# Spatial-stage z1 blocks loaded one quad ahead and gated inside the quad; LayerNorm squares of four rows sent behind the first copies of the z1 quads

## The chip, the cores and the metric

The kernel runs on one core of one Trainium2 chip. The metric is device time in microseconds (us), lower is better. Timed executions of the kernel before took 697.17, 697.22, 698.55 and 698.75 us. The profile is a trace of one execution. That execution has a time of its own.

## The reference, cut to what matters

```python
g = sigmoid((x * gate_w).sum(-1, keepdims=True))
a = attention(x, wqkv, wo)            # 32 heads, 8 keys each, 2 apart
z = gelu(x @ w_in)                    # 2048 x 3584
z1, z2 = z[..., :1792], layernorm(z[..., 1792:])
s = w_sp @ z2 + b_sp[:, None]         # the "spatial" product, 2048 x 2048 x 1792
b = (z1 * s) @ w_out
return g * a + (1 - g) * b
```

The kernel folds the factor `(1 - g)` into z1 before the last product. It calls this gating.

## The kernel before

Order of the work on TensorE (PE): the z2 columns and q, k, v; then 7 pairs of "z1 quads"; then 14 "spatial quads" (two halves `c` of 7); then 8 output quads. A quad is one level of Strassen's scheme: seven block products that accumulate in four PSUM banks. ScalarE (ACT) copies banks to seed others, VectorE (DVE) makes the operand sums and evicts the results. Quads alternate between two sets of four banks.

```python
def strassen(...):
    X, Y, Z, V = bank_roles[quad[0] % 2]
    ...
    product(X, A11 x B11);              nc.scalar.copy(Y, X)      # "first copy"
    product(V, S1 x T1);                share(vs, V)
    product(Y, S2 x T2);                nc.scalar.copy(Z, Y)
    product(X, A12 x B21);              c11(X)
    product(Y, S3 x T3);                nc.scalar.copy(V, Y); c22(Y)
    product(Z, S4 x B22);               c12(Z)
    product(V, A22 x T4);               c21(V)
```

Ahead of the z1 quads there are four dummy matmuls. They write banks 1, 2, 5 and 6, each of which must first be emptied by a GELU of the z2 columns (in the profile of before two of them waited 4.3 us for these). LayerNorm needs the sums of squares of z2. Those of rows 12 to 15 (tiles of 128 rows) are written in the program behind the z1 quads, but they have no order of their own, and the compiler placed them among the last GELUs of the z2 columns (in the profile of before they start from 289.94 to 302.02 us, the GELUs end at 301.9):

```python
for b in (1, 2, 5, 6):
    nc.tensor.matmul(banks[b], xT[:, 4, 0:P], xT[:, 4, 0:512], start=True, stop=True)
for fp in range(NFH):
    ...                                                          # cut
    run(z1_quad(fp, 0), z1_quad(fp, 1), hooks=...)
    if fp < 4:
        junk = free(A_OFF + 16384, FH)      # scratch: shares memory with a block of v that DVE reads
        for x in range(2):
            nc.scalar.activation(junk[...], z2[:, 12 + fp, x * HF:(x + 1) * HF], ACT.Square, accum_out=s2h[...])
```

The spatial quad, where a z1 block is loaded, gated in place, multiplied with the quad's result and stored from the same slot (two slots in turn):

```python
def spatial_quad(c, fp):
    n = quad[0]
    z1t, zgt, zt, vs = z1_slots[n % 2], zg_slots[n % 2], zt_slots[n % 2], v_slots[n % 2]
    for a in range(2):
        sync.dma_start(z1t[:, :, a, :], src)                     # z1 load
    first = sums4(...)                                           # operand sums of this quad
    with tc.high_priority():
        gated = nc.vector.tensor_tensor(zgt, z1t, om, ALU.mult)  # the gate
    if c == 1 and fp == 0:
        wsp_sums(1, 1)              # the last two of the weight sums: T2 and T4 of the second half
    ...
    def c11(X): nc.vector.tensor_tensor(zt[:, 0, 0, :], X[:], b1, ALU.add)
    ...                             # c22, c12 and c21: additions, products with zgt, then four stores
```

Between the spatial quads of the first half, pairs of transposing loads fetch the spatial weights of the second half through the same DMA queue.

Of the kernel before, what the change touches and what calls it, by code (L numbers as in the profile page):

```python
# [9 lines left out]
F32 = mybir.dt.float32  # L10
# [3 lines left out]
P = 128  # L14
# [11 lines left out]
FH = 1792  # L26
NF = FH // P
# [8 lines left out]
HF = FH // 2  # L36
NFH = NF // 2
# [5 lines left out]
A_OFF = X_OFF + 16384  # L43
# [10 lines left out]
def kernel(  # L54
# [13 lines left out]
    nc = tc.nc  # L68
# [4 lines left out]
    sm = ctx.enter_context(tc.tile_pool(name="small", bufs=1))  # L73
# [19 lines left out]
    z1_d = dpool.tile([4, P, NF * 512], BF, name="z1_d")  # L93
# [14 lines left out]
    g_att = sm.tile([P, NJ], F32, name="g_att")  # L108
    s1 = sm.tile([P, 64], F32, name="s1")
    s2 = sm.tile([P, 16], F32, name="s2")  # L110
    s2h = sm.tile([P, 8], F32, name="s2h")
    mean = sm.tile([P, 16], F32, name="mean")
    var = sm.tile([P, 16], F32, name="var")
    rstd = sm.tile([P, 16], F32, name="rstd")
# [274 lines left out]
    def square(i):  # L389
        inst = nc.scalar.activation(junk, z2[:, i, :], ACT.Square, accum_out=s2[:, i:i + 1])  # L390
        tc.add_manual_dep(inst.ins, last_evac[0].ins.name, NOSYNC, reason="behind the banded evacuations")

    def normalize(i):
        sl = slice(i, i + 4)
        s1v = s1[:, 4 * i:4 * (i + 4)].rearrange("p (i c) -> p i c", c=4)
        first = nc.vector.tensor_reduce(mean[:, sl], s1v, AX.X, ALU.add)
        tc.add_manual_dep(first.ins, last_add[0].ins.name, NOSYNC, reason="behind the additions of the quads")
        nc.vector.tensor_scalar(mean[:, sl], mean[:, sl], 1.0 / FH, None, ALU.mult)
        nc.vector.tensor_tensor(var[:, sl], mean[:, sl], mean[:, sl], ALU.mult)
        nc.vector.scalar_tensor_tensor(var[:, sl], s2[:, sl], 1.0 / FH, var[:, sl], ALU.mult, ALU.subtract)  # L400
        nc.vector.tensor_scalar(var[:, sl], var[:, sl], 0.0, EPS, ALU.max, ALU.add)
        nc.gpsimd.tensor_tensor(rstd[:, sl], var[:, sl], cm05[:, sl], ALU.pow)
        for ii in range(i, i + 4):
            nc.vector.tensor_scalar(z2h[:, ii, :], z2[:, ii, :], mean[:, ii:ii + 1], rstd[:, ii:ii + 1],
                                    ALU.subtract, ALU.mult)

    for i in range(16):
        if i > 5:
            for c in range(1, 4):
                z2_tile(i, c)  # L410
        if i < 12:
            square(i)

    def free(off, n, dt=BF):
        r = reg(off, n)
        return r if dt == BF else r.bitcast(dt)
# [35 lines left out]
    def strassen(A11, A12, A22, S1, S2, S3, S4, B11, B21, B22, T1, T2, T3, T4, vs, c11, c12, c21, c22, share=nc.scalar.copy):  # L452

        X, Y, Z, V = bank_roles[quad[0] % 2]
        bank_roles[quad[0] % 2] = [X, Z, V, Y]
        quad[0] += 1
        product(X, list(zip(A11, B11)), True)
        nc.scalar.copy(Y[:], X[:])  # L458
        yield
        product(V, list(zip(S1, T1)), True)  # L460
        with tc.high_priority():
            share(vs, V[:])  # L462
        yield
        product(Y, list(zip(S2, T2)), False)
        nc.scalar.copy(Z[:], Y[:])  # L465
        yield
        product(X, list(zip(A12, B21)), False)
        with tc.high_priority():
            c11(X)
        yield  # L470
        product(Y, list(zip(S3, T3)), False)
        seed = nc.scalar.copy(V[:], Y[:])  # L472
        with tc.high_priority():
            tc.add_manual_dep(c22(Y).ins, seed.ins.name, SYNC, reason="one reader of a bank at a time")
        yield
        product(Z, list(zip(S4, B22)), False)
        with tc.high_priority():
            c12(Z)
        yield
        product(V, list(zip(A22, T4)), False)  # L480
        with tc.high_priority():
            c21(V)
        yield

    def run(*quads, hooks={}):
        quads = list(quads)
        n = 0
        while quads:
            n += 1
            if n in hooks:  # L490
                hooks[n]()
            for q in list(quads):
                if next(q, 0) == 0:
                    quads.remove(q)
# [8 lines left out]
        return first  # L503

    last_add = [None]
    last_share = [None]
    last_store = [None]
    wait_for = [None, None, None]
# [21 lines left out]
    def x_sums(r):  # L530
        for c in range(2):
            lo, hi = slice(512 * c, 512 * c + 512), slice(1024 + 512 * c, 1536 + 512 * c)
            a, b = ((xT[:, 0:4, hi], xT[:, 0:4, lo]), (xT[:, 4:8, hi], xt1[:, :, lo]),
                    (xT[:, 4:8, hi], xT[:, 0:4, hi]), (xT[:, 4:8, lo], xt2[:, :, lo]))[r]
            with tc.high_priority():
                inst = nc.vector.tensor_tensor((xt1, xt2, xt3, xt4)[r][:, :, lo], a, b, ALU.subtract)
            if r == 0:
                tc.add_manual_dep(inst.ins, last_sub[0].ins.name, NOSYNC, reason="behind the softmax maxima")
            if r == 3:
                tc.add_manual_dep(inst.ins, last_share[0].ins.name, NOSYNC, reason="behind the shared terms")  # L540
# [14 lines left out]
    def z1_quad(fp, c):  # L555
        w, s, z1s, vs = w1_slots[fp % 3], ws_slots[fp % 2], z1s_slots[c], zv_slots[c]
        lo, hi = slice(512 * c, 512 * c + 512), slice(1024 + 512 * c, 1536 + 512 * c)

        def share(*a):
            last_share[0] = nc.vector.tensor_copy(*a)  # L560

        def gelu(f, a, bank):
            return nc.scalar.activation(z1s[:, f, a, :], bank[:], ACT.Gelu_apprx_tanh)  # L563

        def add(bank):
            last_add[0] = nc.vector.tensor_tensor(bank[:], bank[:], vs, ALU.add)
            return last_add[0]

        def c22(Y):
            inst = add(Y)  # L570
            gelu(1, 1, Y)
            return inst

        def c12(Z):
            add(Z)
            gelu(0, 1, Z)

        def c21(V):
            gelu(1, 0, V)
            for a in range(2):  # L580
                dst = z1_d[c + 2 * a].rearrange("p (f t) -> p f t", f=NF)[:, fp:fp + NFH + 1:NFH, :]
                last_store[0] = sync.dma_start(dst, z1s[:, :, a, :])

        K4 = range(4)
        return strassen([w[:, k, 0, :] for k in K4], [w[:, 4 + k, 0, :] for k in K4], [w[:, 4 + k, 1, :] for k in K4],
                        *[[s[:, q, k, :] for k in K4] for q in range(4)],
                        [xT[:, k, lo] for k in K4], [xT[:, 4 + k, lo] for k in K4], [xT[:, 4 + k, hi] for k in K4],
                        [xt1[:, k, lo] for k in K4], [xt2[:, k, lo] for k in K4], [xt3[:, k, lo] for k in K4],
                        [xt4[:, k, lo] for k in K4], vs, lambda X: gelu(0, 0, X), c12, c21, c22, share=share)

    for fp in range(3):
        load_w1(fp)
    w1_sums(0)
# [4 lines left out]
    for fp in range(NFH):  # L598
        if fp + 1 < NFH:
            w1_sums(fp + 1)  # L600
        for a in ((), (0,), (1, 2), (3, 4), (5, 6), (7,), ())[fp]:
            load_raw(0, a)
        if fp == 6:
            wsp_sums(0, 0)
        run(z1_quad(fp, 0), z1_quad(fp, 1), hooks={2: lambda: x_sums(2), 4: lambda: x_sums(3)} if fp == 0 else {})
        if fp < 4:
            junk = free(A_OFF + 16384, FH)
            for x in range(2):
                nc.scalar.activation(junk[:, x * HF:(x + 1) * HF], z2[:, 12 + fp, x * HF:(x + 1) * HF], ACT.Square,  # L609
                                     accum_out=s2h[:, 4 * x + fp:4 * x + fp + 1])  # L610
        if 1 <= fp <= 4:
            if fp == 4:
                nc.vector.tensor_tensor(s2[:, 12:16], s2h[:, 0:4], s2h[:, 4:8], ALU.add)
            normalize(4 * fp - 4)
        if fp + 3 < NFH:
            load_w1(fp + 3)

    def spatial_quad(c, fp):
        n = quad[0]
        raw = raw_slots[c].rearrange("p i a t -> p i (a t)")  # L620
        half, t_sum = raw_bits[c], t_sums[c]
        z1t, zgt, zt, vs = z1_slots[n % 2], zg_slots[n % 2], zt_slots[n % 2], v_slots[n % 2]
        for a in range(2):
            src = z1_d[c + 2 * a].rearrange("p (f t) -> p f t", f=NF)[:, fp:fp + NFH + 1:NFH, :]
            sync.dma_start(z1t[:, :, a, :], src)
        lo, hi = slice(fp * P, (fp + 1) * P), slice(HF + fp * P, HF + (fp + 1) * P)
        s = s_slots[n % 2]
        first = sums4([s[:, r] for r in range(4)], z2h[:, 0:8, lo], z2h[:, 8:16, lo], z2h[:, 0:8, hi], z2h[:, 8:16, hi])
        om = _sub_ap(omg_bc, 512 * c, [[0, 2], [1024, 2], [1, 512]])
        with tc.high_priority():  # L630
            gated = nc.vector.tensor_tensor(zgt, z1t, om, ALU.mult)  # L631
        if c == 1 and fp == 0:
            wsp_sums(1, 1)
        if c == 1 and fp == 1:
# [1 line left out]
        b1, b2 = bsp_bc[:, 512 * c:512 * c + 512], bsp_bc[:, 1024 + 512 * c:1536 + 512 * c]  # L636

        def c11(X):
            nc.vector.tensor_tensor(zt[:, 0, 0, :], X[:], b1, ALU.add)

        def c22(Y):
            nc.vector.tensor_tensor(vs, vs, b2, ALU.add)
# [184 lines left out]
```

## Time and profile before

| | kernel before |
|---|---|
| timed executions | 697.17 to 698.75 us |
| the profiled execution | 704.6 us (span 702.8 us) |
| PE busy in the profile | 681.7 us, 97% of the span |
| PE idle ahead of the z1 quads | 4.3 us |
| PE idle in the first quad of the second spatial half | 4.5 us |

The page of the profile of before: the totals by engine (busy us, share of the span, instructions), then the rows of PE's busy tenths and of its granted clock, in 40 slices of the span.

```profile
span 702.8 us, 9358 instructions
PE 681.7 (97%) x3623; PEld 320.8 (46%) x3623; DVE 407.1 (58%) x551; ACT 313.7 (45%) x563; POOL 6.1 (1%) x15
...
PE   6999999999999999889999999997999999999997
...
PEclk9999999999999999989999999998999999999999
```

PE is the bound, busy for 97% of the span: only its idle or slow time can be won. Both rows show dips near slices 17 to 18 and 28. The view of waits of the kernel before names them (engine, what it wrote, line, what it waited for: us in total, times, longest):

```profile
PE psum_all L201 <- DMA arena<-in_A_x_dram: 6.1, 2, 3.6
PE psum_all L449 <- DVE arena L523: 4.5, 1, 4.5
PE psum_all L597 <- ACT arena L223: 4.3, 2, 3.3
```

L597 is the line of the dummies, L223 the z2 GELUs, L523 the last weight sum. A table of windows of the kernel before shows the price of the idle time (columns: stretch in us; its length; busy us and instructions of PE, PE's weight loads, DVE, ACT and POOL; granted clock; DMA share; GB/s):

```profile
296.00:300.00 4.00, 0.66 (x4) 0.22 (x3) 3.64 (x4) 3.91 (x13) 0.00 (x0) 0.90 0.79 223
300.00:304.00 4.00, 2.99 (x7) 0.87 (x7) 0.16 (x1) 3.19 (x9) 0.00 (x0) 0.50 0.00 0
304.00:308.00 4.00, 4.00 (x15) 1.62 (x14) 1.11 (x2) 0.98 (x2) 0.00 (x0) 0.75 0.00 0
484.00:488.00 4.00, 0.16 (x1) 0.00 (x0) 3.96 (x5) 0.00 (x0) 0.00 (x0) 0.86 0.82 263
488.00:492.00 4.00, 3.37 (x8) 1.20 (x9) 4.00 (x7) 0.00 (x0) 0.00 (x0) 0.50 0.98 273
492.00:496.00 4.00, 4.00 (x16) 1.69 (x15) 4.00 (x8) 0.57 (x1) 0.00 (x0) 0.78 0.79 255
```

The clock is the column after POOL's. Around each stall the granted clock is 0.50 for 6.83 us (299.16 to 305.99 and 486.90 to 493.72): the first matmuls of the quads start 0.43 us apart, at full clock 0.216.

The timeline of ACT in the kernel before, around the first stall (start us, length us, engine, line, operation; in brackets the idle time ahead of it and what ended that):

```profile
282.61 0.54 ACT L223 ACTIVATE arena<-psum_all 128x448 bf16<-128x448 f32 x1
...
289.94 0.95 ACT L609 ACTIVATE arena<-arena 128x896 bf16<-128x896 bf16 x1 [6.70 <-issue]
...
291.82 0.52 ACT L223 ACTIVATE arena<-psum_all 128x448 bf16<-128x448 f32 x1
...
292.47 0.95 ACT L609 ACTIVATE arena<-arena 128x896 bf16<-128x896 bf16 x1
...
301.36 0.53 ACT L223 ACTIVATE arena<-psum_all 128x448 bf16<-128x448 f32 x1
...
302.02 0.95 ACT L609 ACTIVATE arena<-arena 128x896 bf16<-128x896 bf16 x1
```

ACT stands still for 6.7 us ahead of the first square (L609). "issue" means that the profile saw nothing to wait for, but the square does wait: its semaphore wait lasts 7.37 us and ends when DVE finishes its 4.42 us product that started at 285.44, the last reader of the memory that the scratch shares. Nine GELUs are then behind, with squares between them.

The timeline of DVE in the kernel before, around the second stall:

```profile
476.43 0.68 DVE L639 TENSOR_TENSOR arena<-psum_all,arena 128x512 f16<-128x512 f32 x1
482.02 1.23 DVE L631 TENSOR_TENSOR arena<-arena 128x2048 f16<-128x2048 bf16 x1 [4.92 <-DMA arena<-z_d]
483.17 0.68 DVE L643 TENSOR_TENSOR arena<-psum_all,arena 128x512 f16<-128x512 f32 x1
...
485.69 0.68 DVE L650 TENSOR_TENSOR arena<-psum_all,arena 128x512 f16<-128x512 f32 x1
486.30 2.28 DVE L523 TENSOR_TENSOR arena<-arena 128x4096 f16<-128x4096 bf16 x1
```

L631 is the gate. It waits 4.9 us for its z1 load, in front of evictions and the weight sum L523 (2.28 us). The first of those evictions, L643, belongs to the quad before: the copy that it follows was made at 470.44, some 12 us earlier, so DVE is almost a quad late. PE ran out of work at 484.16, waiting for that sum.

### The profile page before, as it was taken

To read this page: it belongs to the slowest core of one execution; us is meant where nothing else is said; L and a number is where in the kernel's file an instruction comes from. 1 tells how busy PE (TensorE), PEld (TensorE's weight loads), DVE (VectorE), ACT (ScalarE), POOL (GpSimd) and SP (SyncE) were. 2 spreads that over 40 slices of the span, in tenths; PEclk is the share of its full clock that TensorE was granted. 3 is DMA by queue.
4 is the path that set the end of the run, shared out by engine and by line. 5 is a ranking of instruction groups with operands and counts; after the bars stand their busy time and mean duration, and the time that the engine had idled before them with its cause. 6 is when DMAs were issued, how large, how long until landed. Compare 5 with 4: busy or idle time off the path is not lost.

```text
span 702.8 us, 9358 instructions
## 1 busy us (share of the span) xinstructions
PE 681.7 (97%) x3623; PEld 320.8 (46%) x3623; DVE 407.1 (58%) x551; ACT 313.7 (45%) x563; POOL 6.1 (1%) x15
## 2 busy tenths in 40 slices
PE   6999999999999999889999999997999999999997
PEld 3546544645444455434444444443444444444443
DVE  1000171977699969945677965497767694523301
ACT  4436457564768799666666311211111211112121
POOL 1000000000000000000010000000000000000000
PEclk9999999999999999989999999998999999999999
DMA  9995557485588570107986368838555388964200
GB/s 226 219 273 154 148 173 214 125 233 128 178 245 224 145 160 1 53 23 197 207 212 177 110 135 151 156 83 237 148 120 162 100 195 191 190 145 98 55 35 30
DMA packets 241740, 106.45 MB, mean 151 GB/s; under 512 B 189712, under 2 KB 235168, under 8 KB 241696
## 3 DMA queue, kind: packets, MB, share of 16 engines
q1 hardware_dynamic: 241008, 105.33, 60.1%
q8 instruction: 28, 0.46, 0.3%
q10 hardware_dynamic: 688, 0.53, 0.2%
q14 instruction: 16, 0.13, 0.1%
HBM read 45.10 MB, written 45.00 MB: 128 GB/s over the span
## 4 chain that ended last, share of the span: by engine, by line
PE 73%; DVE 9%; DMA 8%; SPq 4%; ACT 3%; issue 2%; DVEq 0%; ACTq 0%
PE psum_all L449 41%; PE psum_all L256 15%; PE psum_all L263 8%; PE psum_all L221 7%; DMA arena<-z_d 3%; SPq L188 3%; DVE arena L340 2%; PE psum_all L292 2%; DVE arena L631 1%; SPq L183 1%; DMA band_d_73<-arena 1%; ACT arena L609 1%; ACT arena L223 1%; DMA band_d_75<-arena 1%; DMA arena<-in_A_x_dram 1%
## 5 line engine op out<-in xcount | busy, mean ns | idle before, releaser
L449 PE MATMUL psum_all<-arena 128*128 128x512 f16 (+1 forms) x1792 | 392.2, 382 | 4.8 <-DVE arena L523 4.5
L449 PEld LDWEIGHTS <-arena 128*128 128x128 f16 (+1 forms) x1792 | 176.2, 98 | 222.2 <-issue 8.7
L256 PE MATMUL psum_all<-arena 128*128 128x512 bf16 x512 | 116.2, 380 | 0.0
L221 PE MATMUL psum_all<-arena 128*128 128x448 bf16 (+1 forms) x512 | 101.4, 357 | 0.4 <-ACT arena L223 0.4
L340 DVE TENSOR_TENSOR arena<-arena,att_A 128x8192 f16<-128x8192 bf16 x16 | 70.7, 4421 | 6.3 <-DMA arena<-v_d 6.1
L256 PEld LDWEIGHTS <-arena 128*128 128x128 bf16 x512 | 47.5, 98 | 56.6 <-issue 0.2
L221 PEld LDWEIGHTS <-arena 128*128 128x128 bf16 x512 | 49.7, 99 | 47.5 <-issue 2.6
L340 DVE TENSOR_TENSOR arena<-arena 128x4096 f16<-128x4096 f16 (+2 forms) x48 | 67.3, 1402 | 1.4
L297 ACT CAST arena<-psum_all 128x1620 f16<-128x1620 f32 (+2 forms) x48 | 65.1, 1356 | 3.7 <-DMA band_d_73<-arena 2.4
L458 ACT COPY psum_all<-psum_all 128x512 f32<-128x512 f32 x36 | 20.5, 570 | 89.3 <-PE psum_all L449 72.2
L263 PE MATMUL psum_all<-arena 128*128 128x512 bf16 x256 | 57.5, 381 | 0.0
L258 ACT CAST arena<-psum_all 128x512 bf16<-128x512 f32 x64 | 37.3, 586 | 40.6 <-PE psum_all L256 39.1
L465 ACT COPY psum_all<-psum_all 128x512 f32<-128x512 f32 x36 | 20.5, 570 | 53.6 <-PE psum_all L449 53.6
L263 PEld LDWEIGHTS <-arena 128*128 128x128 bf16 x256 | 36.1, 145 | 18.1
L472 ACT COPY psum_all<-psum_all 128x512 f32<-128x512 f32 x36 | 20.5, 571 | 50.2 <-PE psum_all L449 50.2
L223 ACT ACTIVATE arena<-psum_all 128x448 bf16<-128x448 f32 x64 | 34.4, 545 | 17.7 <-PE psum_all L221 17.7
L498 DVE TENSOR_TENSOR arena<-arena 128x512 f16<-128x512 bf16 (+2 forms) x37 | 20.6, 564 | 34.9 <-DMA arena<-zg_d 17.1
L563 ACT ACTIVATE arena<-psum_all 128x512 bf16<-128x512 f32 x56 | 31.8, 598 | 6.9 <-PE psum_all L449 3.6
L501 DVE TENSOR_TENSOR arena<-arena 128x512 f16<-128x512 bf16 (+2 forms) x37 | 20.5, 562 | 23.7 <-PE psum_all L449 13.0
L631 DVE TENSOR_TENSOR arena<-arena 128x2048 f16<-128x2048 bf16 x14 | 17.1, 1223 | 29.3 <-DMA arena<-z_d 28.6
L266 ACT CAST arena<-psum_all 128x512 bf16<-128x512 f32 x32 | 18.6, 585 | 26.3 <-PE psum_all L263 26.3
L462 ACT COPY arena<-psum_all 128x512 f32<-128x512 f32 x22 | 12.8, 587 | 36.2 <-PE psum_all L449 33.3
(86 smaller groups left out, 346.7 us busy)
## 6 DMA issues: line engine op xcount, KB each, us to landing
arena<-v_d SPq DMA_DIRECT2D x8, 960.0 KB, 6.0
z_d<-arena SPq DMA_DIRECT2D x28, 256.0 KB, 2.6
arena<-z_d SPq DMA_DIRECT2D x28, 256.0 KB, 3.5
zg_d<-arena SPq DMA_DIRECT2D x56, 128.0 KB, 2.3
arena<-zg_d SPq DMA_DIRECT2D x32, 224.0 KB, 3.4
arena<-in_A_wqkv_dram SPq DMA_DIRECT2D x16, 256.0 KB, 4.7
v_d<-arena SPq DMA_DIRECT2D x32, 128.0 KB, 2.6
o_d<-arena SPq DMA_DIRECT2D x4, 1024.0 KB, 5.8
```

Of the source, the lines that this page charges most:

```text
L188: inst = _orig_dmat(*a, **k)
L221: nc.tensor.matmul(ps[:, 0:N], xT[:, kt, i * P:(i + 1) * P], w2[:, kt, w2_off[c]:w2_off[c] + N], start=(kt == 0), stop=(kt == KT - 1))
L223: inst = nc.scalar.activation(z2[:, i, ZC * c:ZC * (c + 1)], ps[:, 0:ZC], ACT.Gelu_apprx_tanh, accum_out=s1[:, 4 * i + c:4 * i + c + 1])
L256: nc.tensor.matmul(ps[:], w[:, t, kt, :], xT[:, kt, 512 * c:512 * (c + 1)], start=(kt == 0), stop=(kt == KT - 1))
L258: nc.scalar.copy(dst[:, :, 256 * c:256 * (c + 1)], ps[:].rearrange("p (n e) -> p e n", e=2))
L263: nc.tensor.matmul(ps[:], _sub_ap(xT_flat, kt * S + j, [[NJ, P]]), wv[:, kt, 512 * hf:512 * hf + 512], start=(kt == 0), stop=(kt == KT - 1))
L297: evac = nc.scalar.copy(dst, src)
L340: inst = nc.vector.tensor_tensor(*a)
L449: nc.tensor.matmul(bank[:], lhsT, rhs, start=(start and m == 0), stop=(stop and m == n - 1), skip_group_check=True)
L498: first = nc.vector.tensor_tensor(s_out[0], a21, a22, ALU.add)
L563: return nc.scalar.activation(z1s[:, f, a, :], bank[:], ACT.Gelu_apprx_tanh)
L631: gated = nc.vector.tensor_tensor(zgt, z1t, om, ALU.mult)
```

## The change: its intent, and the diff

The squares go behind the first copies of the first four z1 pairs, where ACT has a gap. The z1 load of quad n+1 is asked for in quad n, and the gate moves into the quad, behind the eviction that follows the fourth product. The work is the same.

```diff
         product(X, list(zip(A11, B11)), True)
-        nc.scalar.copy(Y[:], X[:])
+        last_seed[0] = nc.scalar.copy(Y[:], X[:])
 ...
+    def between(fp):                      # run as a hook after the first products of the pair
+        if fp == 0:
+            x_sums(2)
+        row = SQ0 + fp                    # SQ0 = 12
+        if row < 16:
+            junk = free(A_OFF + 16384, FH)
+            for x in range(2):
+                sq = nc.scalar.activation(junk[...], z2[:, row, x * HF:(x + 1) * HF], ACT.Square, accum_out=s2h[...])
+                tc.add_manual_dep(sq.ins, last_seed[0].ins.name, NOSYNC, reason="behind the first copies of the quads")
 ...
-        if fp < 4:
-            ...                           # the squares behind the quads, as above
 ...
+    def load_z1(n):
+        c, fp = divmod(n, NFH)
+        for a in range(2):
+            src = ...
+            sync.dma_start(z1_slots[n % 2][:, :, a, :], src)
+
     def spatial_quad(c, fp):
-        n = quad[0]
+        n = NFH * c + fp
+        if n == 0:
+            load_z1(0)
+        if n + 1 < 2 * NFH:
+            load_z1(n + 1)
 ...
-        for a in range(2):
-            ...                           # the z1 load
 ...
-        with tc.high_priority():
-            gated = nc.vector.tensor_tensor(zgt, z1t, om, ALU.mult)
 ...
         def c11(X):
-            nc.vector.tensor_tensor(zt[:, 0, 0, :], X[:], b1, ALU.add)
+            inst = nc.vector.tensor_tensor(zt[:, 0, 0, :], X[:], b1, ALU.add)
+            gated = nc.vector.tensor_tensor(zgt, z1t, om, ALU.mult)
+            tc.add_manual_dep(gated.ins, inst.ins.name, NOSYNC, reason="in this order")
```

Cut: a wider `s2h` and the addition of its halves.

More of the change, by code (lines that the diff above doesn't have):

```diff
@@ L110 @@
     s2 = sm.tile([P, 16], F32, name="s2")
-    s2h = sm.tile([P, 8], F32, name="s2h")
+    s2h = sm.tile([P, 16], F32, name="s2h")
     mean = sm.tile([P, 16], F32, name="mean")
@@ L391, in square @@
         tc.add_manual_dep(inst.ins, last_evac[0].ins.name, NOSYNC, reason="behind the banded evacuations")
+    SQ0 = 12
     def normalize(i):
@@ L410 @@
                 z2_tile(i, c)
-        if i < 12:
+        if i < SQ0:
             square(i)
@@ L505 @@
     last_add = [None]
+    last_seed = [None]
+    last_gelu = [None]
     last_share = [None]
@@ L562, in gelu @@
         def gelu(f, a, bank):
-            return nc.scalar.activation(z1s[:, f, a, :], bank[:], ACT.Gelu_apprx_tanh)
+            last_gelu[0] = nc.scalar.activation(z1s[:, f, a, :], bank[:], ACT.Gelu_apprx_tanh)
         def add(bank):
@@ L589, in z1_quad @@
                         [xt4[:, k, lo] for k in K4], vs, lambda X: gelu(0, 0, X), c12, c21, c22, share=share)
+    def between(fp):
[5 more added lines that the diff above has]
+            for x in range(2):
+                sq = nc.scalar.activation(junk[:, x * HF:(x + 1) * HF], z2[:, row, x * HF:(x + 1) * HF], ACT.Square,
+                                          accum_out=s2h[:, 8 * x + row - 8:8 * x + row - 7])
+                tc.add_manual_dep(sq.ins, last_seed[0].ins.name, NOSYNC, reason="behind the first copies of the quads")
     for fp in range(3):
@@ L604 @@
             wsp_sums(0, 0)
-        run(z1_quad(fp, 0), z1_quad(fp, 1), hooks={2: lambda: x_sums(2), 4: lambda: x_sums(3)} if fp == 0 else {})
-        if fp < 4:
-            junk = free(A_OFF + 16384, FH)
-            for x in range(2):
-                nc.scalar.activation(junk[:, x * HF:(x + 1) * HF], z2[:, 12 + fp, x * HF:(x + 1) * HF], ACT.Square,
-                                     accum_out=s2h[:, 4 * x + fp:4 * x + fp + 1])
-        if 1 <= fp <= 4:
-            if fp == 4:
-                nc.vector.tensor_tensor(s2[:, 12:16], s2h[:, 0:4], s2h[:, 4:8], ALU.add)
-            normalize(4 * fp - 4)
+        run(z1_quad(fp, 0), z1_quad(fp, 1), hooks={2: lambda: between(fp), 4: lambda: x_sums(3) if fp == 0 else None})
+        if 1 <= fp <= 4:
+            n = 4 * fp - 4
+            a = max(n, SQ0)
+            if n + 4 > SQ0:
+                nc.vector.tensor_tensor(s2[:, a:n + 4], s2h[:, a - 8:n - 4], s2h[:, a:n + 4], ALU.add)
+            normalize(n)
         if fp + 3 < NFH:
             load_w1(fp + 3)
-    def spatial_quad(c, fp):
-        n = quad[0]
+    def load_z1(n):
+        c, fp = divmod(n, NFH)
+        for a in range(2):
+            src = z1_d[c + 2 * a].rearrange("p (f t) -> p f t", f=NF)[:, fp:fp + NFH + 1:NFH, :]
+            sync.dma_start(z1_slots[n % 2][:, :, a, :], src)
+    def spatial_quad(c, fp):
+        n = NFH * c + fp
[3 more added lines that the diff above has]
+            load_z1(n + 1)
         raw = raw_slots[c].rearrange("p i a t -> p i (a t)")
@@ L622, in spatial_quad @@
         z1t, zgt, zt, vs = z1_slots[n % 2], zg_slots[n % 2], zt_slots[n % 2], v_slots[n % 2]
-        for a in range(2):
-            src = z1_d[c + 2 * a].rearrange("p (f t) -> p f t", f=NF)[:, fp:fp + NFH + 1:NFH, :]
-            sync.dma_start(z1t[:, :, a, :], src)
         lo, hi = slice(fp * P, (fp + 1) * P), slice(HF + fp * P, HF + (fp + 1) * P)
```

## The prediction

> **What bounds the kernel now.** TensorE: the page gives PE 681.7 us busy of a span of 702.8 us (97%; VectorE/DVE 58%, ScalarE/ACT 45%). Only PE's idle and slow time can be won. The view of waits lists the idle time: 6.1 us at the start, 4.3 us for the dummy matmuls just before the z1 quads (for GELU evictions on ACT), 4.5 us in the first quad of the second spatial half (for the last sum of the spatial weights, on DVE), 2 us of small ones. The two middle stalls also cost clock: the table of windows shows 0.50 from 300 to 304 us and 0.64 from 488 to 496 us.
>
> **What each stall costs in all.** A z1 pair or spatial quad takes 12.09 us where PE is fed (spacing of ACT's first copies in the timeline).
> - First: without it the quads would start at about 296.8, not 301.9 (5.1 us), and the first pair loses 2.07 us at half clock. Sum 7.2 us.
> - Second: first copies at 475.56 and 494.80, 19.24 us instead of 12.09: 7.15 us.
>
> [...] after stalls of 3.3+1.0 and 4.5 us, matmuls come 0.43 us apart instead of 0.216.
>
> **Why, and what the change does.**
> 1. The squares of rows 12 to 15 sit in ACT's queue among the last GELUs. The first waits for DVE to leave the scratch region (ACT idle 6.7 us until 289.94); nine GELUs (0.54 us) pile up behind, interleaved with eight squares (0.95 us each). The change sends the squares behind the first copies of the first four z1 pairs. There ACT idles 1.97 us; two squares take 1.88 us. A copy some tenths late is harmless: the bank is needed three products (2.6 us) later. I expect the whole 7.2 us.
> 2. The gating of quad n+1 (1.22 us) stands ahead of quad n's tail on DVE and waits for its load (28.6 us over 8 waits). That load waits for the stores of quad n-1, which follow that tail: a loop of 14 to 15 us per quad while weight transposes (5.2 us) stand in the same queue, against PE's 12.09. DVE falls some 10 us behind, and the last weight sum (2.28 us), behind a gate that waited 4.9 us, comes late. After, the load is asked for a quad ahead and the gate stands some 7 us into the quad; DVE's 8 us per quad plus weight sums fit. I expect the whole 7.15 us, and a 0.3 us wait near 392 us too.
>
> The work is unchanged: same squares, loads, gates, bytes.
>
> **Prediction.** In the profile -14.4 us, span about 688.5. Timed, 697.2 - 14.4 = 682.8 if the stalls are as profiled; but timed runs are 7 us shorter than the profiled one, so stalls or half-clock stretches may be smaller there, and I take a little off: **683.6 us, range 680.8 to 690**. Faster by over 2%: 0.45; within 2%: 0.53; slower: 0.02.
>
> **Right if** PE's waits no longer show the dummies on ACT nor the weight sum on DVE; granted clock is 1.0 from 290 to 690 us; squares come in pairs after first copies; first copies of spatial quads are 12.09 us apart throughout; DVE's wait for z1 loads falls from 28.6 to under 5 us; PE busy falls by about 4.5 us (no half-clock matmuls).
>
> **Wrong if** the scheduler orders queues otherwise (squares delaying copies that PE needs, a z1 load behind a blocked DMA entry, gate 0 late); if a remaining wait exceeds 3 us and the clock still drops; or if without the profiler the stalls are much shorter, which leaves 3 to 8 us.

One sentence of the prediction and the clause after it are cut, as the mark shows; they gave for the idle time that halves the clock a figure that this case does not show. The forecast's 14.4 us are 7.2 + 7.15 us, rounded, taken off the 702.8 us span and the timed 697.2 us. The half clock after the two stalls, part of both terms, is measured in the profile of before.

## The result, and the profile after

| | before | after |
|---|---|---|
| timed, median | 697.88 us | 689.86 us |
| timed, range (4 executions each) | 697.17 to 698.75 | 689.41 to 690.32 |
| profiled execution, span | 702.8 us | 687.3 us |
| PE busy | 681.7 us | 671.8 us |

The ratio is 0.9884, with a 95% interval of 0.9867 to 0.9902. Ratios in this document are the mean time of one kernel's fast runs over that of the other's fast runs of the same rounds, so they are not quite the ratios of the medians quoted. The timed gain is 8.0 us, the gain between the two profiles 15.5 us.

The page of the profile after, same lines:

```profile
span 687.3 us, 9315 instructions
PE 671.8 (98%) x3566; PEld 319.9 (47%) x3623; DVE 409.2 (60%) x551; ACT 314.1 (46%) x563; POOL 6.2 (1%) x15
...
PE   6999999999999999999999999999999999999997
...
PEclk9999999999999999999999999999999999999999
```

No dip is left in the busy tenths, and the clock is full (1.000 over the span). (PE's busy time fell by 9.9 us, but this profile holds 57 matmul records fewer, at the same number of weight loads. A second profile of the changed kernel, in experiment 9, holds all 3623 and has 676.8 us: 4.9 us less than before, about what the prediction expected of matmuls that no longer run at half clock.) The waits of PE after (two lines of the form "issue", 2.1 us together, are left out; the complete profile of experiment 9 does not have them):

```profile
PE psum_all L201 <- DMA arena<-in_A_x_dram: 5.9, 2, 3.6
...
PE psum_all L292 <- ACT arena L297: 0.8, 3, 0.3
PE psum_all L221 <- ACT arena L223: 0.4, 1, 0.4
PE psum_all L451 <- DVE arena L662: 0.2, 1, 0.2
```

The windows after, for the stretches that held the stalls:

```profile
296.00:300.00 4.00, 3.95 (x19) 1.86 (x19) 3.80 (x5) 2.58 (x5) 0.00 (x0) 1.00 0.50 142
300.00:304.00 4.00, 4.00 (x21) 1.75 (x19) 3.36 (x5) 2.80 (x7) 0.00 (x0) 1.00 0.02 4
484.00:488.00 4.00, 4.00 (x20) 1.86 (x19) 3.21 (x5) 0.57 (x1) 0.00 (x0) 1.00 0.36 123
488.00:492.00 4.00, 3.95 (x20) 1.78 (x19) 3.05 (x5) 0.57 (x1) 0.00 (x0) 1.00 0.30 65
```

ACT's timeline after: the GELUs keep pace with PE (each waits some 0.9 us for it), and the squares (L602) sit between the first and the second copies (L460, L467):

```profile
295.34 0.54 ACT L223 ACTIVATE arena<-psum_all 128x448 bf16<-128x448 f32 x1 [0.88 <-PE psum_all L221]
...
297.12 0.57 ACT L460 COPY psum_all<-psum_all 128x512 f32<-128x512 f32 x1 [1.15 <-PE psum_all L451]
297.99 0.57 ACT L460 COPY psum_all<-psum_all 128x512 f32<-128x512 f32 x1 [0.29 <-PE psum_all L451]
298.47 0.95 ACT L602 ACTIVATE arena<-arena 128x896 bf16<-128x896 bf16 x1
...
299.41 0.94 ACT L602 ACTIVATE arena<-arena 128x896 bf16<-128x896 bf16 x1
...
300.52 0.57 ACT L467 COPY psum_all<-psum_all 128x512 f32<-128x512 f32 x1
```

DVE's timeline after, where the last weight sum is made (L657 is the gate, L527 the sum):

```profile
460.72 0.68 DVE L656 TENSOR_TENSOR arena<-psum_all,arena 128x512 f16<-128x512 f32 x1
461.32 1.22 DVE L657 TENSOR_TENSOR arena<-arena 128x2048 f16<-128x2048 bf16 x1
462.45 0.68 DVE L503 TENSOR_TENSOR arena<-arena 128x1024 f16<-128x1024 f16 x1
...
465.42 0.69 DVE L669 TENSOR_TENSOR arena<-psum_all,arena 128x512 f16<-128x512 f32 x1 [0.31 <-PE psum_all L451]
466.03 2.28 DVE L527 TENSOR_TENSOR arena<-arena 128x4096 f16<-128x4096 bf16 x1
```

This gate does not wait; over all gates DVE waits 1.2 us for z1 loads, once, where it waited 28.6 us before. The sum starts 83.2 us after the first copy of the first spatial quad (382.81); before, it started 95.8 us after it (486.30 against 390.51). In the kernel before PE ran out of work 93.65 us after that copy (484.16 less 390.51), so the 2.28 us sum has to start by about 91 us. After, it has some 8 us to spare.

### The profile page after: what moved, and what is told of

Same layout as the page of the kernel before. It is cut to its first block, busy times and chain, and to the rows that moved or that the text cites. A ratio compares the mean times of both kernels' runs of the same rounds, so it can differ in the third digit from the quotient of the medians.

```text
span 687.3 us, 9315 instructions
## 1 busy us (share of the span) xinstructions
PE 671.8 (98%) x3566; PEld 319.9 (47%) x3623; DVE 409.2 (60%) x551; ACT 314.1 (46%) x563; POOL 6.2 (1%) x15
## 4 chain that ended last, share of the span: by engine, by line
PE 89%; DVE 6%; ACT 2%; DMA 1%; issue 1%; SPq 0%; ACTq 0%; DVEq 0%
PE psum_all L451 55%; PE psum_all L221 13%; PE psum_all L256 11%; PE psum_all L263 8%; DVE arena L340 4%; PE psum_all L292 1%; DMA arena<-in_A_x_dram 1%; ACT arena L297 1%; ACT arena L390 0%; ACT arena L223 0%; DMA arena<-o_d 0%; PE psum_all L201 0%; ACT arena L258 0%; DVE arena L662 0%; ACT att_L_107 L319 0%
## 5 line engine op out<-in xcount | busy, mean ns | idle before, releaser
L451 PE MATMUL psum_all<-arena 128*128 128x512 f16 (+1 forms) x1758 | 385.6, 379 | 2.0 <-DVE arena L662 0.2
L256 PE MATMUL psum_all<-arena 128*128 128x512 bf16 x495 | 113.9, 380 | 1.7 <-issue 1.3
L460 ACT COPY psum_all<-psum_all 128x512 f32<-128x512 f32 x36 | 20.5, 570 | 80.7 <-PE psum_all L451 78.9
L263 PE MATMUL psum_all<-arena 128*128 128x512 bf16 x250 | 56.3, 380 | 0.9 <-issue 0.8
L467 ACT COPY psum_all<-psum_all 128x512 f32<-128x512 f32 x36 | 20.5, 570 | 48.6 <-PE psum_all L451 48.3
L502 DVE TENSOR_TENSOR arena<-arena 128x512 f16<-128x512 f16 (+2 forms) x37 | 20.5, 565 | 7.9 <-PE psum_all L451 7.5
```

What stands on the lines that cost most here:

```text
L256: nc.tensor.matmul(ps[:], w[:, t, kt, :], xT[:, kt, 512 * c:512 * (c + 1)], start=(kt == 0), stop=(kt == KT - 1))
L263: nc.tensor.matmul(ps[:], _sub_ap(xT_flat, kt * S + j, [[NJ, P]]), wv[:, kt, 512 * hf:512 * hf + 512], start=(kt == 0), stop=(kt == KT - 1))
L451: nc.tensor.matmul(bank[:], lhsT, rhs, start=(start and m == 0), stop=(stop and m == n - 1), skip_group_check=True)
```

## The experiments

Each kernel was timed against the kernel before on the same chip. Experiments 1 to 4 shared one chip and its runs of the kernel before; 5, 7 and 8 shared a second; 6 and 9 a third. All results were correct except where it is said. The record counts every timed run as fast, that is, undisturbed; "long" and "short" below are executions of one kernel that differ within that.

### 1. Only the loads asked for one quad ahead

```diff
+        if n + 1 < 2 * NFH:
+            load_z1(n + 1)
 ...
-        for a in range(2):
-            ...
-            sync.dma_start(z1t[:, :, a, :], src)
```

> Only the loads are asked for one quad ahead; the gate keeps its place. The compiler places every instruction and wait on every queue exactly as before, so this is also a second copy of the kernel before. If asking earlier mattered by itself (my prediction's reading of part 2), it would win some 4 to 7 us; since the program is the same, ratio 1.000 within 0.2%. It also shows what the executions of the kernel before look like: if the profile of before caught half-clock stretches that most executions lack, the others have a mean clock of 1.00 and spans of 695 to 697 us, and the profile here shows both stalls (some 4 us each) but less or no half clock; if the rival holds (in other executions the stalls themselves are short), PE's waits on ACT and on the weight sum are together under 4 us here.

Measured: 697.88 us against 697.2 us, ratio 0.9995 (0.9955 to 1.0034). The traces of the two hold the same work on every engine and the same transfers in the DMA queue, in the same order. So this half of the change does nothing by itself: a load waits for the stores of the quad two before, which free its slot, and between those stores and the load the queue still holds the transposes (in the profile of before four stores are issued from 401.53 us, two transposes from 403.85 us, the loads from 409.21 us; experiment 7 puts the load ahead of them). With the gate moved it is no different: the queue of experiment 2, which lacks this half, issues the same transfers in the same order as that of the changed kernel.

This second look at the program of before is not like the first. Its waits of PE:

```profile
PE psum_all L597 <- ACT arena L223: 4.0, 2, 2.9
PE psum_all L449 <- DVE arena L523: 1.7, 1, 1.7
```

The first stall is the same (4.0 us, and half clock: the 33 matmuls from 301.17 us take 9.14 us, 0.28 us each on average, against 0.216 at full clock). The second is 1.7 us instead of 4.5, and no half clock follows it (the 71 matmuls from 484.34 us take 15.93 us, 0.22 us each). The span is 696.1 us instead of 702.8. The profile that I predicted from had caught one of the long executions: in this call the 11 timed executions of the kernel before lie between 696.29 and 703.96 us. By the spacing of the first copies (19.24 and 13.97 us against 12.09) the second stall cost 7.15 us there and 1.88 us here. The expectation that half clock alone made the difference was wrong: some 2.8 us of it are the stall itself, some 2.5 us the half clock. Nor did its rival hold as stated: the two waits come to 5.7 us, not under 4.

### 2. Only the gate moved

```diff
-        with tc.high_priority():
-            gated = nc.vector.tensor_tensor(zgt, z1t, om, ALU.mult)
 ...
+            gated = nc.vector.tensor_tensor(zgt, z1t, om, ALU.mult)      # in c11, behind the eviction
```

> Only the gate is moved behind the fourth product's eviction; loads and squares as before. If the gate's place ahead of the tail closed the loop that made DVE late, the stall on the last weight sum (4.5 us in the profile of before) and DVE's 28.6 us of waits for z1 loads vanish here, and the time falls by 3.5 to 7 us (ratio 0.990 to 0.995), with the stall before the z1 quads left. If the load ahead was needed too, the waits for z1 loads stay over 10 us and the time falls by under 2 us.

Measured: 696.68 us (695.08 to 697.07), ratio 0.9968 (0.9933 to 1.0003). DVE's wait for z1 loads falls from 25.9 us (experiment 1) to 1.2 us, PE's wait for the weight sum is gone, and the first stall stays at 4.3 us. (The compiler also ordered other DVE instructions and some transfers of the spatial stage differently, so the gate is not all that moved.) The mechanism is as expected, the size is below it: 0.5 us by the medians, 2.2 us by the means, and the interval reaches past 1. The longest execution is 697.07 us, where the kernel before reached 703.96 us on the same chip.

### 3. Only the squares moved

The edit is the first half of the diff of the change; the spatial stage is as before.

```diff
+                sq = nc.scalar.activation(junk[...], z2[:, row, x * HF:(x + 1) * HF], ACT.Square, accum_out=s2h[...])
+                tc.add_manual_dep(sq.ins, last_seed[0].ins.name, NOSYNC, reason="behind the first copies of the quads")
 ...
-        if fp < 4:
-            ...                           # the squares behind the quads
```

> Only the squares are moved behind the first copies of the quads; the spatial stage is as before. The wait of the dummy matmuls on ACT (4.3 us) vanishes, the stall on the last weight sum stays. Time falls by 3.5 to 7 us (ratio 0.990 to 0.995). If the two parts are independent, the gains of this run and of the gate moved alone add up to that of the whole change, 8 us; if not, their sum differs by over 2 us.

Measured: 690.78 us (689.90 to 692.32), ratio 0.9889 (0.9854 to 0.9924). That is 6.4 us by medians, 7.7 us by the means. The dummies no longer wait, and the mean granted clock of the profiled execution is 0.999. PE's wait for the last weight sum is 1.7 us. So the squares give most of the timed gain. Their gain and that of the gate come to 0.9857 as a product of ratios; the whole change had 0.9884 on one chip and has 0.9834 on another (experiment 9), so the two parts look independent within what these intervals can tell.

### 4. The squares in their old place, with a free scratch region

The rival to "the wait for the scratch" is "the squares' own 7.5 us among the GELUs". The order of ACT's instructions was pinned to that of before; only the memory that the squares write differs. (The compiler then moved a few small DVE instructions.)

```diff
-            junk = free(A_OFF + 16384, FH)
+            scr = reg(CD_OFF + 512 + 16384 + 4096 + 8192, FH)      # held by nobody at that time
 ...                                  # cut: the dependencies that pin ACT's order
```

> The squares stay where they were in ACT's queue, instruction for instruction, but write to a scratch region that nobody holds, so that the first of them need not wait for DVE. If the wait for the scratch region made the stall, ACT no longer idles 6.7 us ahead of the squares, GELUs keep pace with PE (per row three GELUs and two squares take 3.4 us of ACT against 4.5 us of PE), the dummies wait under 0.7 us, and the gain is that of moving the squares, within 1 us. If the squares' own 7.5 us among the GELUs made it, the dummies still wait over 3 us and the ratio is 0.998 to 1.000.

Measured: 690.35 us, ratio 0.9878 (0.9842 to 0.9914). ACT's timeline in this kernel (L224 GELU, L420 square):

```profile
282.52 0.54 ACT L224 ACTIVATE arena<-psum_all 128x448 bf16<-128x448 f32 x1
...
283.04 0.96 ACT L420 ACTIVATE arena<-arena 128x896 bf16<-128x896 bf16 x1
...
283.97 0.95 ACT L420 ACTIVATE arena<-arena 128x896 bf16<-128x896 bf16 x1
...
284.90 0.54 ACT L224 ACTIVATE arena<-psum_all 128x448 bf16<-128x448 f32 x1
...
296.70 0.95 ACT L420 ACTIVATE arena<-arena 128x896 bf16<-128x896 bf16 x1
```

The squares run between the GELUs as before, but the first starts at once, and PE never waits for the dummies. The gain is that of moving the squares. So the stall was the wait for memory that DVE held, not the squares' work. Another scratch address would have done as much as moving them.

### 5. PE kept busy through the first stall

```diff
-    for b in (1, 2, 5, 6):
+    for b in (1, 2) + 16 * (2,) + (5, 6):
         nc.tensor.matmul(banks[b], xT[:, 4, 0:P], xT[:, 4, 0:512], start=True, stop=True)
```

> The kernel before, with 16 more dummy matmuls (about 3.5 us) where TensorE waited for ACT ahead of the z1 quads; every queue but PE's is unchanged. ACT still lets the last dummy go at the same time, so the idle time's place is filled but not shortened. If 2.07 us of the first stall are the half clock that follows idle time, the clock stays 1.0 from 296 to 306 us, the first z1 pair takes 12.1 us instead of 14.15, and the time falls by about 2 us (ratio 0.997). If half clock there has another cause, it comes all the same and the time stays within 0.3 us of that of before or above it.

Measured: 699.8 us (695.91 to 702.06) against 696.59, ratio 1.0027 (0.9993 to 1.0062): the time did not fall, against my expectation. The clock did what was expected. Windows of this kernel:

```profile
300.00:304.00 4.00, 2.88 (x15) 1.18 (x13) 0.16 (x1) 3.86 (x10) 0.00 (x0) 1.00 0.00 0
304.00:308.00 4.00, 4.00 (x20) 1.85 (x19) 3.43 (x5) 1.39 (x4) 0.00 (x0) 1.00 0.02 4
484.00:488.00 4.00, 3.30 (x9) 1.25 (x10) 4.00 (x7) 0.00 (x0) 0.00 (x0) 0.57 0.87 273
```

It is 1.00 from 300 to 308 us. The quads start at 301.61, and the first copy of the second pair comes at 314.81, 13.2 us later; before it was 15.24 us (301.89 to 317.13). So 2.0 us were won there. (The expectation's 3.5 us for 16 matmuls is an estimate, from the 0.216 us between matmuls in the profile of before; here the 16 and the first three took 4.26 us.) In this profile they were more than lost again in the second stall, which is now 3.3 us, with some 3.4 us of half clock (0.57 is the mean of the 4 us from 484 us, and from 488 us it is 1.00): first copies 17.09 us apart, so it cost 5.0 us where it cost 1.88 us in experiment 1. The last weight sum started 94.2 us after the first spatial copy, 1.6 us later than in experiment 1. The profile is not alone: four of the six executions have a mean granted clock of 0.995 or 0.996, the other two (695.91 and 696.49 us) 0.999. Whether the earlier start of the quads lengthens the second stall, or it was long by chance, no run isolates.

### 6. The same, with the gate moved

```diff
-    for b in (1, 2, 5, 6):
+    for b in (1, 2) + 16 * (2,) + (5, 6):
 ...
-            gated = nc.vector.tensor_tensor(zgt, z1t, om, ALU.mult)      # ahead of the quad
+            gated = nc.vector.tensor_tensor(zgt, z1t, om, ALU.mult)      # in c11, behind the eviction
```

> The gate moved (so that the stall on the last weight sum can't take back what is won earlier) and the 16 extra dummies in the idle time ahead of the z1 quads. If the clock is worth 2 us there and the extra dummies alone won nothing only because the second stall grew, this run is about 2 us faster than the gate moved alone (695.1 to 697.1): 693.5 to 695, ratio 0.995 to 0.996, with the clock at 1.0 from 290 to 690 us. If half clock costs nothing that the time shows, it stays at the gate's ratio, 0.997 to 0.9985.

Measured: 694.03 us (693.66 to 695.41), ratio 0.9904 (0.9873 to 0.9935). The mean granted clock of the profiled execution is 1.000 and PE's wait for the weight sum is gone. The medians differ by 2.65 us from the gate alone (696.68 us, on another chip). The ratio itself is not the one expected, because on this chip the kernel before took 697.91 to 703.8 us. The changed kernel took 689.32 us on the same chip: the 4.7 us between them (4.1 us in the two profiles, by the first copy of the z1 quads: 301.87 against 297.77) are the idle time of the first stall without its half clock.

### 7. The z1 load ahead of the transposes, gate in its old place

```diff
+            load_z1(n + 1)
+        if 1 <= n <= 4:
+            for a in (2 * n - 2, 2 * n - 1):
+                tc.add_manual_dep(load_raw(1, a).ins, last_z1[0].ins.name, NOSYNC, reason="behind the z1 block")
 ...                                  # cut: the transposes at their old place, behind the quad
```

> The gate keeps its old place ahead of the tail, but the z1 load goes into the DMA queue ahead of the weight transposes. If the loop store, transposes, load, gate, tail made DVE late, taking 5 us of transposes out of it brings it under PE's 12.09 us: DVE's waits for z1 loads fall from 25 to 29 us to under 10 us and the stall on the last weight sum is under 0.5 us; time falls by 0.8 to 1.8 us (ratio 0.9975 to 0.999). If the gate's place alone is what counts, waits and stall stay as before. A later arrival of the transposes may give some of it back through the weight sums.

Measured: 695.67 us (694.92 to 696.25), ratio 0.9978 (0.9956 to 0.9999). The stall on the weight sum is gone, and the sum starts 84.7 us after the first spatial copy. DVE's waits for z1 loads fall to 13.7 us, not under 10. In the DMA queue the pairs of z1 loads now come 12.0 to 12.5 us apart (402.93, 415.16, 427.15, 439.61), about PE's 12.09 us per quad; before they came 13.8 to 15.6 us apart (409.21, 424.81, 439.81, 453.64). (The compiler also placed the gates a few DVE instructions earlier, never later.) So shortening the loop removes the stall too: the lag came from the loop of store, transposes, load, gate and tail, as the prediction had it.

### 8. Every transpose of the second half twice, before and after

```diff
             load_raw(1, a)
+            load_raw(1, a)
```

> The kernel before, with each of the eight weight transposes of the second half issued twice, which puts about 5 us more into the loop in each of the first four quads. If DVE's lag comes from that loop, it grows by up to 5 us a quad: the stall in the first quad of the second half grows to between 5 and 20 us, with half clock, or others appear in the quads before it, and the time rises by 5 to 20 us. If the stall has nothing to do with the queue, time stays within 1 us. (The compiler also orders a few DVE instructions otherwise.)

> The same doubling on the changed kernel. If the gate's new place takes the load's delay off the tail, the stores stay on time and no stall over 2 us appears in the spatial stage: ratio 0.988 to 0.992 to the kernel before, as for the change without doubling. If the new place only hides a small delay, it stalls as the doubled kernel before does.

Measured: before with doubling 701.02 us (697.17 to 704.88), ratio 1.0055 (1.0012 to 1.0097); after with doubling 689.58 us (689.28 to 689.85), ratio 0.9890. The second is as expected: at its gates DVE waits 0.4 us for z1 loads and 2.3 us for stores in all. The first is a miss: the stall on the sum is 3.8 us, no more than in the long execution of the kernel before, where I had expected 5 to 20 us. The compiler had placed the gates and the stores otherwise: at its gates DVE waited only 12.4 us for z1 loads, but 15.6 us for stores, in all as long as before. So this pair shows that the changed kernel stands some 10 us of transposes per quad (four took 9.4 to 10.8 us to issue); it says little about the loop.

### 9. The change again, and with narrow dummies

> The changed kernel once more, on the same chip as the others of this call: ratio 0.988 to 0.990; no PE wait of over 1 us after the start.

Measured: 689.32 us (689.10 to 690.03), ratio 0.9834 (0.9801 to 0.9867). No PE wait after the start is over 1 us. The changed kernel takes the same time as in its first measurement; the kernel before took 701.52 us in the median here, against some 697 us on the others. The larger gain is the kernel before taking longer.

```diff
-        nc.tensor.matmul(banks[b], xT[:, 4, 0:P], xT[:, 4, 0:512], start=True, stop=True)
+        nc.tensor.matmul(banks[b][:, 448:512], xT[:, 4, 0:P], xT[:, 4, 0:64], start=True, stop=True)
```

> The changed kernel with its four dummy matmuls 64 columns wide instead of 512 (448 to 511, the only columns of these banks that the matmuls before may not have written). If results stay correct, the z1 quads start about 0.75 us sooner after the last z2 matmul [...], and the time falls by that: 0.1%, hardly to be told from noise by time, but to be read from the trace. If the dummies had to write whole banks, results are wrong.

Measured: wrong results (relative error 0.38), at 688.85 us. So 64 columns are not enough here; why, no run shows. (The 0.75 us of the expectation is the author's estimate; its working is cut, as the mark shows. In the profile of before matmuls of 448 columns, the width saved, start 0.189 us apart: four are 0.76 us.) It is not a usable version. No experiment gave a correct kernel clearly faster than the changed one.

## Why the prediction was right or wrong

**Right in range.** 689.86 us lies in the range of 680.8 to 690, and the class was the likelier of the two named. But the point of 683.6 us is 6.3 us too low, and the range held by 0.14 us, less than the spread of the four timings, two of which (690.25 and 690.32) lie above it: that it held is partly luck. One of its own conditions for being wrong came true, too: the second stall is much shorter in most timed runs, as far as experiment 1 and the granted clocks of the record show, and the gain of 8.0 us is the top of the "3 to 8 us" named for that case.

**The first stall: right, in cause and size.** It was predicted at 7.2 us, of which 2.07 us half clock. Squares alone: 6.4 to 7.7 us. Half clock by itself: 2.0 us in the trace of experiment 5, 2.65 us by the medians of 6 and 2 (on two chips); idle time by itself: 4.7 us (experiment 6 against the change). Experiment 4 shows that the wait for the scratch was the cause. The squares in their new place cost PE nothing, as predicted: the second copies come at 300.52 us, and PE waits for none of them.

**The second stall: right in mechanism, wrong in size.** This is the term that failed: "I expect the whole 7.15 us". It was read from one execution of 704.6 us, when the timed ones took 697 to 699 us. In another execution of the same program it was 1.7 us without half clock. Alone, the gate's move was worth 0.5 us by medians and 2.2 us by means, because only the long executions lose more; what it buys above all is a steady time. The mechanism stands: experiments 2 and 7 remove the stall by different cuts in the same loop.

**"The load is asked for a quad ahead": this step is wrong.** Asking earlier changes no order of instructions or transfers (experiment 1). What this half of the change won, it won by moving the gate.

**The doubt about the profile: right, but taken too lightly.** The prediction said that timed runs were 7 us shorter and that stalls may be smaller there, and took off 0.8 us. It had the number to find it: 704.6 less 697.2 is close to the whole second stall (7.15 us), so much of the stall was likely to be missing from the timed runs. In the profiles the prediction (-14.4 us) did hold: -15.5 us. About 0.8 us of the rest is an earlier arrival at the dummies (295.14 against 295.94), ahead of anything that the change moves.

**Idle time and the clock, and the order of the queues.** In the profile of before, a wait of 3.3 us (1.0 us more followed) and one of 4.5 us brought half clock: the granted clock fell at 299.16 and 486.90 us, 2.96 and 3.12 us after PE's last matmul had started (296.20 and 483.78), for 6.83 us each time. In experiment 5 a single wait of 3.3 us brought some 3.4 us of it; in experiment 1 a wait of 1.7 us brought none. What the shortest such wait is, and what sets the length of the stretch, these runs do not show. In the profile of before, ACT and DVE did not pass over an instruction that waited: DVE idled 4.9 us before a gate while the eviction L643 behind it had had its input for some 11 us, and ACT idled 6.7 us before a square with finished GELU inputs behind it.

**What stays open.** Why one execution of the same program has the long second stall and another the short one: the start of the sum, counted from the first spatial copy, varied from 91.7 to 95.8 us over the profiles with the old gate and the old order of loads, and the DMA times in the loop vary (a pair of transposes took 4.2 to 5.6 us to issue), but no run isolates the cause. That all executions above 700 us are such cases is an inference from three things: the profiled one was; no kernel whose profile lacks the second stall took over 697.07 us; and of the 33 timed executions of the kernel before in these experiments, the nine above 700 us have mean granted clocks of 0.989 to 0.993, the other 24 of 0.994 to 0.998. (Half clock is not all of it: one execution of experiment 1 took 700.31 us at 0.995.)

## What to carry to other kernels

Before costing a stall from a profile, compare the profiled execution's own time with the timed ones; if they differ by about the stall, the stall may be absent from most runs. An operation that waits must not stand ahead of ones that others need in a queue that does not pass it over, as ACT's (6.7 us idle before a square) and DVE's (4.9 us before a gate) did not here: giving it another scratch address, or another place, can be worth more than its own duration (a square takes 0.95 us; the other address won 6.85 us by the medians of experiment 4). A request written earlier in the program does nothing if a buffer, and not the request, sets its time (experiment 1: ratio 0.9995).
